# The end of a four-layer attention kernel: the last unit's exponentials, an output projection taken earlier, and unread matmuls in the last waits

## The chip, the cores and the metric

The kernel runs on one core of a Trainium2 chip. The metric is the device time of one execution in microseconds (us). The times before are three runs: 2391.03, 2398.66 and 2393.85 us, so the median is 2393.85. The profiled execution took 2389.35 us, and its span from the first to the last instruction is 2387.6 us; every time below that is a place on the profile's clock counts from the start of this span.

The engines are named as in the profile: PE is TensorE (matmuls) and PEld its weight loads, ACT is ScalarE (exponentials), DVE is VectorE (elementwise work), POOL is GpSimd and SP the engine that issues most of the transfers.

## The reference

One sequence of 2048 rows and 640 columns passes through four residual attention layers, A, B, A, B. Each has 32 heads of 20 columns. In A a query sees only the 256 keys up to itself; in B it sees all 2048.

```python
qkv = x @ wqkv                      # x normalised row by row first
scores = q @ k.T * (Dh ** -0.5)     # per head
p = softmax(scores)                 # A: only where 0 <= i - j < 256
o = p @ v
return o.reshape(B, S, D) @ wo

x = x + A(layernorm(x))
x = x + B(layernorm(x))
x = x + A(layernorm(x))
x = x + B(layernorm(x))
```

Layers are counted 0 to 3. The change touches only the end of layer 3, a full attention.

## The kernel before

**Units, banks, tiles.** The queries are cut into 4 chunks of 512 (`c`), the heads into 8 groups of 4 (`g`), the keys into 16 blocks of 128. A *unit* (l, c, g) is the attention of one chunk in one head group. The last two units are (3, 3, 6) and (3, 3, 7). A unit's scores are computed block by block: for one key block and one head of the group, one matmul (line 1186) fills one PSUM bank of 128 keys x 512 queries. Heads lie 32 rows apart, so that the matmuls of one block use different rows of TensorE. ScalarE turns three or four banks at a time into exponentials (line 1206), reading one group of banks while TensorE fills the other: banks 0 to 2 in even tiles, banks 3 to 5 or 3 to 6 in odd ones. Four-bank tiles exist only where no other work is waiting for bank 6 (`next_tile`). Their output tile is called `ka` in the profile, since it lies in an old key buffer; three-bank tiles write `pt`. A little later four matmuls (line 1238), one for each head, multiply the exponentials with the values and accumulate in bank 7 (`op`), 21 rows to a head: 20 columns of output and the sum of the exponentials.

**The side path.** In layer 3, from chunk 1 on, most units leave their last key block, number 15, to VectorE (`self.aside`). A score matmul (line 837) fills bank 6, and twelve VectorE operations (lines 843 to 881) compute the exponential of two heads from the bits of the number and a polynomial. A unit needs this twice, so 24 operations. The result is multiplied with the values by line 1247, two matmuls for each pair of heads, which end the accumulation in `op`. The planner emits these four matmuls where the unit ends, so everything behind them on TensorE waits until VectorE is done.

**The end of a unit.** `finish_unit` copies `op` to `oT` (line 805), and `t_tail` normalises it: the sums are gathered with four matmuls (line 967), their reciprocal is taken and split in two halves (lines 972 to 977), transposed (982), copied (984), spread over the heads' rows with four matmuls (991), and multiplied into `on` (995). `on` holds the normalised outputs of the 8 head groups of a chunk.

**The output projection.** `t_out` multiplies the 8 groups of `on` with `wo`, for 4 row blocks times 2 halves of the columns: 8 outputs of 8 matmuls with 320 columns (line 529), each added to x on VectorE (line 538). For the last chunk it is split: `t_before_last` takes groups 0 to 6 as soon as the tail of unit (3, 3, 6) is done (8 outputs of 7 matmuls, line 560) and adds x (line 568), into the buffer `raw_o`. `t_out` then has only group 7 left, adds `raw_o`, and stores four blocks of rows (line 544).

**What sets the order.** The order on every engine is written by a planner while the program is built: it emits one tile of scores and exponentials after another, and after each tile gives waiting tasks (`todo`, and first of all `tails`) a little work from a credit (`pump`). A task that needs a PSUM bank calls `take_m`; in this stage only bank 6 is to be had. After the last value product the planner frees banks 0 to 5 as well and emits whatever tasks are left. The planner's counts aren't times of the chip; each engine runs its instructions in the written order and waits on semaphores.

In an earlier stage, `keep_clock` (line 612) issues matmuls whose results nothing reads, so that TensorE's clock isn't lowered. It isn't used in layer 3 after chunk 0.

Of the kernel before, what the change touches and what calls it, by code (L numbers as in the profile page):

```python
# [22 lines left out]
G = 8  # L23
C = 512
NC = S // C
# [24 lines left out]
def kernel(  # L50
# [10 lines left out]
    nc = tc.nc  # L61
# [34 lines left out]
    ident = big.tile([P, P], BF16, name="ident", tag="ident")  # L96
# [3 lines left out]
    masks = big.tile([P, 3, C], BF16, name="masks", tag="masks")  # L100
# [7 lines left out]
    ps = psp.tile([P, 8, C], F32, name="ps", tag="ps")  # L108
# [20 lines left out]
    def load_wop(w):  # L129
        v = wo_in[w].rearrange("(g j e) f -> j e g f", g=G, j=4)  # L130
        for j in range(4):
            nc.sync.dma_start(out=wop[32 * j : 32 * j + DH, :, :], in_=v[j])
# [46 lines left out]
    class Task:  # L179


        count = 0

        def __init__(self, name, gen, need, left, lead):
            self.name, self.gen, self.need, self.wake = name, gen, need, 0
            self.left = left
            self.holds = False
            Task.count += 1
            self.key = (need - lead, Task.count)
# [60 lines left out]
    mfree = {5: (0, 0), 6: (0, 1)}  # L250
    mseq = [1]

    def take_m():
        while True:
            b = min(mfree, key=mfree.get)
            if mfree[b][0] <= state["tick"]:
                mfree[b] = (1 << 30, 0)
                return b
            yield ("wait", 1)

    def drop_m(b):
        mseq[0] += 1
        mfree[b] = (state["tick"] + (not state["early"]), mseq[0])
# [103 lines left out]
    def stats(l, c, i):  # L367
        if (l, c) not in mvs:
            mvs[l, c] = lnp.tile([P, 4, 2], F32, name="mv", tag="mv")
        st = lnp.tile([P, 2, 6], F32, name="stats", tag="stats")  # L370
        xv = x_sb[:, 4 * c + i, :]
        nc.vector.bn_stats(out=st[:, 0, :], in_=xv[:, 0:HD])
        nc.vector.bn_stats(out=st[:, 1, :], in_=xv[:, HD:D])
        nc.vector.bn_aggr(out=mvs[l, c][:, i, :], in_=st[:])
# [143 lines left out]
    def t_out(l, c):  # L518
        on = ons[l, c]
        last = (l, c) == (3, NC - 1)  # L520
        while last and "before_last" not in ready:
            yield ("wait", 1)
        assert out_seq[out_n[0]] == l % 2
        for qb in range(4):
            for i in range(2):
                mb = yield from take_m()
                yp = ps[:, mb, 0:HD]
                for g in range(G - 1 if last else 0, G):
                    nc.tensor.matmul(  # L529
                        yp, lhsT=on[:, g, qb * P : (qb + 1) * P],  # L530
                        rhs=wop[:, g, i * HD : (i + 1) * HD],
                        start=(last or g == 0), stop=(g == G - 1),
                    )
                    if g < G - 1:
                        yield ("hold", 0.14)
                xv = x_sb[:, 4 * c + qb, i * HD : (i + 1) * HD]
                had = part_o["t"][:, 2 * qb + i, 0:HD] if last else xv
                nc.vector.tensor_tensor(out=xv, in0=had, in1=yp, op=ALU.add)  # L538
                drop_m(mb)
                yield ("pe", 0.14)  # L540
            if l < 3:
                stats(l + 1, c, qb)
            else:
                nc.sync.dma_start(out=xout[:, 4 * c + qb, :], in_=x_sb[:, 4 * c + qb, :])
        ons.pop((l, c))
        ready.add(("out", l, c))
        ready.add(("x", l + 1, c))
        n = out_n[0] = out_n[0] + 1
        if n < len(out_seq) and out_seq[n] != out_seq[n - 1]:
            load_wop(out_seq[n])  # L550

    def t_before_last():

        on = ons[3, NC - 1]
        for qb in range(4):
            for i in range(2):
                mb = yield from take_m()
                yp = ps[:, mb, 0:HD]
                for g in range(G - 1):
                    nc.tensor.matmul(  # L560
                        yp, lhsT=on[:, g, qb * P : (qb + 1) * P],
                        rhs=wop[:, g, i * HD : (i + 1) * HD],
                        start=(g == 0), stop=(g == G - 2),
                    )
                    if g < G - 2:
                        yield ("hold", 0.14)
                xv = x_sb[:, 4 * (NC - 1) + qb, i * HD : (i + 1) * HD]
                nc.vector.tensor_tensor(
                    out=part_o["t"][:, 2 * qb + i, 0:HD], in0=xv, in1=yp, op=ALU.add
                )  # L570
                drop_m(mb)
                yield ("pe", 0.14)
        ready.add("before_last")
# [44 lines left out]
    def key_blocks(l, part):  # L618
        return part or (0, NT)

    class Unit:
        def __init__(self, l, c, g, part=None):
            self.l, self.c, self.g, self.part = l, c, g, part
            self.windowed = l % 2 == 0
            self.aside = False
            if self.windowed:
                sets = [(m, b0, subs, j) for m, b0, subs in window_banks(c) for j in range(4)]
            else:
                self.aside = l == 3 and c > 0 and (c, g) != (1, 0)
                k0, k1 = key_blocks(l, part)  # L630
                kcs = range(k0, k1 - self.aside)
                sets = [(None, 0, [(kc, 0, 4, 0)], j) for kc in kcs for j in range(4)]
            n = len(sets)
            self.banks = [
                (self, j, m, b0, subs, i < 4, i >= n - 4 and not self.aside, i == n - 1)
                for i, (m, b0, subs, j) in enumerate(sets)
            ]
# [322 lines left out]
            live["va"] -= 2 + 2 * (u.c > 0) + 2 * (u.c == NC - 1)  # L960

    def t_tail(l, c, g, on, oT):
        yield ("wait", 2)
        mb = yield from take_m()
        zp = ps[:, mb, 0:16]
        for qb in range(4):
            nc.tensor.matmul(
                zp[:, 4 * qb : 4 * qb + 4], lhsT=oT[:, qb * P : (qb + 1) * P],
                rhs=sel4[:], start=True, stop=True,
            )  # L970
        rz = rzp.tile([P, 16], F32, name="rz", tag="rz")
        nc.vector.reciprocal(out=rz[:], in_=zp)
        drop_m(mb)

        hl = rzp.tile([P, 2, 16], BF16, name="hl", tag="hl")
        nc.vector.tensor_copy(out=hl[:, 0, :], in_=rz[:])
        nc.vector.tensor_tensor(out=hl[:, 1, :], in0=rz[:], in1=hl[:, 0, :], op=ALU.subtract)
        yield ("pe", 0.25)
        yield ("wait", 2)
        mb = yield from take_m()  # L980
        rp = ps[0:32, mb, :].bitcast(BF16)[:, 0:P]
        nc.tensor.transpose(out=rp, in_=hl[:].rearrange("p n r -> p (n r)"), identity=ident[:])  # L982
        rT = rzp.tile([32, P], BF16, name="rT", tag="rT")
        nc.vector.tensor_copy(out=rT[:], in_=rp)  # L984
        drop_m(mb)
        yield ("pe", 0.1)
        yield ("wait", 2 if state["tick"] < last_tick[0] else 1)
        mb = yield from take_m()
        zb = ps[:, mb, :]
        for qb in range(4):  # L990
            nc.tensor.matmul(  # L991
                zb[:, qb * P : (qb + 1) * P], lhsT=spread4[:, qb, :], rhs=rT[:],
                start=True, stop=True,
            )
        nc.vector.tensor_tensor(out=on[:, g, :], in0=oT[:], in1=zb, op=ALU.mult)  # L995
        drop_m(mb)
        yield ("pe", 0.3)
        ready.add(("tail", l, c, g))
        if (l, c, g) == (3, NC - 1, G - 2):
            push("before_last", t_before_last(), 0, 8.0)  # L1000
        if g == G - 1:
            need = first_use(l + 1, c, 0) if l < 3 else len(units) + c
            push(("out", l, c), t_out(l, c), need, 9.0)
            if l < 3:
                push_layer(l + 1, c)
# [82 lines left out]
    with tc.manual_schedule():  # L1088
# [14 lines left out]
        n = 0  # L1103
# [48 lines left out]
        while ended is None or t < ended + 8:  # L1152
# [3 lines left out]
            if t < len(tiles) or banks:  # L1156
# [26 lines left out]
                for n in range(2):  # L1183
                    for i, (u, j, m, b0, subs, first, last, end) in enumerate(cur):
                        for kc, q0, qn, col in subs[n : n + 1]:
                            nc.tensor.matmul(  # L1186
                                sp[:, i, col * P : (col + qn) * P],
                                lhsT=u.k(kc, j), rhs=u.q(j, q0, qn), start=True, stop=True,
# [39 lines left out]
            if len(pts) >= 4 and pts[3][0] <= t - (3 if pts[0][3][0].windowed else 2):  # L1228
                group = [pts.popleft() for _ in range(4)]
                u, subs, end = group[0][3][0], group[0][3][4], group[3][3][7]  # L1230
                first, last = group[0][3][5:7]
# [3 lines left out]
                for n, (kc, q0, qn, col) in enumerate(subs):  # L1235
                    for _, pg, i, b in group:
# [3 lines left out]
                            lhsT=u.v(kc, j), rhs=pg[:, i, col * P : (col + qn) * P],  # L1240
                            start=(first and n == 0), stop=(last and n == len(subs) - 1),
                            skip_group_check=u.windowed,
                        )
                if end and u.aside:
                    pair = side_done(u)
                    for j in range(4):
                        nc.tensor.matmul(
                            op[32 * j : 32 * j + VW, :], lhsT=u.v(NT - 1, j),
                            rhs=pair[j // 2][:, j % 2, :], start=False, stop=True,
# [21 lines left out]
                        )  # L1271
                    i = k
            masked = (cur, pt) if n_b else None
        mfree.update((b, (0, 0)) for b in range(6))
        state["early"] = True
        while tails or todo:
            state["tick"] += 1
# [31 lines left out]
```

## Time and profile before

| what | value |
|---|---|
| median of three runs | 2393.85 us |
| span of the profiled execution | 2387.6 us |
| ScalarE busy | 2200.7 us, 92% |
| TensorE busy | 1994.0 us, 84% |
| VectorE busy | 1265.8 us, 53% |
| mean granted TensorE clock | 0.808 |
| last exponential ends | 2363.59 us |

A row of groups names the line, engine and operation, the tile written and the tiles read with their shapes, the number of instructions, their busy time and mean duration, and then the idle time just ahead of them with what ended it. A row of the timeline gives the start, the length, the same names, and in brackets the idle time of the engine ahead of it and who released it. In the slices each digit is a fortieth of the span, in tenths. A row of stretches gives from and to, the length, busy time (with the number of instructions) of PE, PEld, DVE, ACT and POOL, then the granted clock, the DMA share and GB/s.

### The profile page before, as it was taken

The numbers are of one execution on the slowest core, as the hardware profiler recorded it, in microseconds if no ns is written. First come the engines' busy times: TensorE is split into PE (matmuls) and PEld (weight loads), VectorE is DVE, ScalarE is ACT, GpSimd is POOL, SyncE is SP. The second block draws the span as 40 slices with busy tenths as digits, with TensorE's granted clock in tenths as the row PEclk, the third lists the DMA queues.
The fourth block names the chain that finished last, engine by engine and source line by source line (L and its number), as shares of the span: only waits on it lengthen the run. The fifth ranks groups of instructions, "written<-read, shape, count | busy, mean of one in ns | idle before, by whom it ended". The sixth has DMA issues, their size and how long they took to land. (4 is left out here: it accounts for less than half of the span.)

```text
span 2387.6 us, 39480 instructions
## 1 busy us (share of the span) xinstructions
PE 1994.0 (84%) x15394; PEld 705.2 (30%) x15539; DVE 1265.8 (53%) x2460; ACT 2200.7 (92%) x1738; POOL 141.2 (6%) x295
## 2 busy tenths in 40 slices
PE   7888988888888798888878888888888788888886
PEld 3443333323322332223322333232222121122112
DVE  6576776423323343423443434442577777777776
ACT  7777889899999999999999999999999999999995
POOL 3111110000000001000100001001000000000000
PEclk9899999978998998889997999789755575557556
DMA  6232422322200232102330124112210010011000
GB/s 182 71 94 70 112 67 59 81 61 65 82 19 26 57 80 83 34 13 57 87 94 16 20 82 109 33 31 76 63 29 26 26 37 26 27 38 37 26 13 12
DMA packets 173676, 132.51 MB, mean 55 GB/s; under 512 B 115760, under 2 KB 156080, under 8 KB 173488
## 3 DMA queue, kind: packets, MB, share of 16 engines
q1 hardware_dynamic: 163872, 101.39, 17.2%
q0 software_dynamic: 9616, 28.59, 3.5%
q8 instruction: 122, 2.00, 0.4%
q14 instruction: 66, 0.54, 0.1%
HBM read 98.70 MB, written 27.79 MB: 53 GB/s over the span
## 5 line engine op out<-in xcount | busy, mean ns | idle before, releaser
L1206 ACT ACTIVATE pt<-ps 128x1536 bf16<-128x1536 f32 (+3 forms) x1586 | 2054.9, 1452 | 127.0 <-PE ps L1186 113.1
L1186 PE MATMUL ps<-qt,kt 32*128 32x512 bf16 x4004 | 659.5, 476 | 230.3 <-ACT pt L1206 169.9
L1238 PE MATMUL ps<-pt,vt 128*21 128x512 bf16 x3744 | 479.2, 469 | 23.1 <-DVE oT L805 13.4
L1186 PEld LDWEIGHTS <-kt 32*128 32x128 bf16 x4004 | 191.3, 94 | 645.9 <-issue 623.6
L1268 DVE TENSOR_TENSOR pt<-pt,masks 128x1024 bf16<-128x1024 bf16 (+5 forms) x403 | 238.7, 626 | 101.8 <-ACT pt L1206 101.0
L353 PE MATMUL ps<-xnT,wqk 128*128 128x512 bf16 x761 | 217.6, 397 | 28.8 <-DMA wqk<-in_B_wqkv_dram 9.6
L1238 PEld LDWEIGHTS <-vt 128*21 128x21 bf16 x4004 | 104.0, 91 | 369.9 <-issue 361.4
L304 DVE CAST st<-ps 128x512 bf16<-128x512 f32 x127 | 87.8, 691 | 199.3 <-PE ps L353 192.3
L612 PE MATMUL ps<-masks,ident 128*128 128x512 bf16 x467 | 173.8, 435 | 4.7 <-issue 3.5
L529 PE MATMUL ps<-wop,on 128*128 128x320 bf16 x968 | 168.9, 318 | 5.9 <-DVE on L995 3.5
L1186 PE MATMUL ps<-qa,ka 32*128 32x384 bf16 (+2 forms) x1408 | 119.6, 282 | 42.7 <-ACT pt L1206 38.1
L995 DVE TENSOR_TENSOR on<-oT,ps 128x512 bf16<-128x512 bf16 x128 | 87.5, 684 | 115.6 <-PE ps L991 113.8
L538 DVE TENSOR_TENSOR x_sb<-x_sb,ps 128x320 bf16<-128x320 bf16 x120 | 58.1, 484 | 146.5 <-PE ps L529 146.3
L843 DVE TENSOR_SCALAR xnT<-ps 128x512 int32<-128x512 f32 x92 | 63.5, 691 | 128.5 <-PE ps L837 125.4
L805 DVE CAST oT<-ps 128x512 bf16<-128x512 f32 x112 | 76.8, 686 | 101.2 <-PE ps L1238 87.4
L1206 ACT ACTIVATE ka<-ps 128x2048 bf16<-128x2048 f32 x65 | 127.3, 1959 | 2.7 <-PE ps L1186 2.2
L444 PE MATMUL ps<-wv,xnT 128*128 128x320 bf16 x640 | 114.5, 313 | 5.3 <-DVE va L304 1.5
L529 PEld LDWEIGHTS <-on 128*128 128x128 bf16 x968 | 89.4, 102 | 72.9 <-issue 37.6
L353 PEld LDWEIGHTS <-wqk 128*128 128x128 bf16 x830 | 72.2, 99 | 123.4 <-issue 51.5
L1238 PE MATMUL ps<-pt,va 128*21 128x384 bf16 (+2 forms) x1408 | 80.2, 291 | 9.8 <-DVE oT L805 4.1
L1186 PEld LDWEIGHTS <-ka 32*128 32x128 bf16 x1408 | 44.3, 92 | 111.4 <-issue 103.4
L984 DVE COPY rT<-ps 32x128 bf16<-32x128 bf16 x128 | 26.8, 209 | 89.4 <-PE ps L982 88.8
(91 smaller groups left out, 1437.5 us busy)
## 6 DMA issues: line engine op xcount, KB each, us to landing
vt<-v_d SPq DMA_DIRECT2D x48, 336.0 KB
kt<-k_d SPq DMA_DIRECT2D x192, 80.0 KB
wqk<-in_B_wqkv_dram SPq DMA_DIRECT2D x80, 160.0 KB
wqk<-in_A_wqkv_dram SPq DMA_DIRECT2D x70, 160.0 KB
k_d<-st POOLq DMA_DIRECT2D x75, 128.0 KB, 2.2
q_d<-st POOLq DMA_DIRECT2D x75, 128.0 KB, 2.0
qt<-q_d SPq DMA_DIRECT2D x384, 20.0 KB
v_d<-vs POOLq DMA_DIRECT2D x16, 336.0 KB, 3.2
```

The lines of the kernel that those rows point to most:

```text
L304: nc.vector.tensor_copy(out=out_, in_=in_)
L353: nc.tensor.matmul(pq, lhsT=wt[:, dc, :], rhs=xt[:, dc, :], start=(dc == 0), stop=(dc == KD - 1),)
L444: nc.tensor.matmul(pv, lhsT=xt[:, dc, i * P : (i + 1) * P], rhs=wv_sb[l % 2][:, dc, h * HD : (h + 1) * HD], start=(dc == 0), stop=(dc == K ...
L529: nc.tensor.matmul(yp, lhsT=on[:, g, qb * P : (qb + 1) * P], rhs=wop[:, g, i * HD : (i + 1) * HD], start=(last or g == 0), stop=(g == G - 1),)
L612: nc.tensor.matmul(ps[:, b, :], lhsT=ident[:], rhs=masks[:, 0, :], start=True, stop=True)
L805: nc.vector.tensor_copy(out=oT[:], in_=op)
L843: V.tensor_scalar(out=xi.bitcast(I32)[:, i * C : (i + 1) * C], in0=ps[:, 6, :], scalar1=SCALE * LOG2E * E23, scalar2=127.0 * E23, op0=ALU. ...
L995: nc.vector.tensor_tensor(out=on[:, g, :], in0=oT[:], in1=zb, op=ALU.mult)
L1186: nc.tensor.matmul(sp[:, i, col * P : (col + qn) * P], lhsT=u.k(kc, j), rhs=u.q(j, q0, qn), start=True, stop=True,)
L1206: nc.scalar.activation(out=pt[:, i:k, b0 * P :], in_=sp[:, i:k, b0 * P :], func=ACT.Exp, scale=SCALE,)
L1238: nc.tensor.matmul(op[32 * j : 32 * j + VW, q0 * P : (q0 + qn) * P], lhsT=u.v(kc, j), rhs=pg[:, i, col * P : (col + qn) * P], start=(first ...
L1268: nc.vector.tensor_tensor(out=pt_[:, i:k, b0 * P :], in0=pt_[:, i:k, b0 * P :], in1=mv_, op=ALU.mult,)
```

## The change

Four edits, all at the end of layer 3.

- The last unit (3, 3, 7) no longer uses the side path: ScalarE computes the exponentials of its key block 15 like the others'. This is meant to take the wait for VectorE out of the end.
- `t_before_last` takes six groups instead of seven, and is started after the tail of unit (3, 3, 5) rather than (3, 3, 6). It then runs while the last units compute, and `t_out` at the end takes the two groups that are left, 16 matmuls instead of 8.
- In the last tail, `fill` issues 2, 3, 1 and 3 matmuls of 128x512 whose result nothing reads, into bank 0, in the places where TensorE waits for VectorE. They are meant to keep TensorE's clock up.
- Bank 0 is left out of the banks that are freed at the end, since the fills write there.

```diff
-                for g in range(G - 1 if last else 0, G):
+                g0 = G - 2 if last else 0
+                for g in range(g0, G):
...
-                        start=(last or g == 0), stop=(g == G - 1),
+                        start=(g == g0), stop=(g == G - 1),
...
-                for g in range(G - 1):
+                for g in range(G - 2):
...
-                        start=(g == 0), stop=(g == G - 2),
+                        start=(g == 0), stop=(g == G - 3),
...
-                    if g < G - 2:
+                    if g < G - 3:
...
-                self.aside = l == 3 and c > 0 and (c, g) != (1, 0)
+                self.aside = l == 3 and c > 0 and (c, g) not in ((1, 0), (NC - 1, G - 1))
...
     def t_tail(l, c, g, on, oT):
+        def fill(count):
+
+            for n in range(count * ((l, c, g) == (3, NC - 1, G - 1))):
+                nc.tensor.matmul(
+                    ps[:, 0, :], lhsT=ident[:], rhs=masks[:, 0, :], start=True, stop=True
+                )
+
         yield ("wait", 2)
+        fill(2)
...
         yield ("pe", 0.25)
+        fill(3)
...
         yield ("pe", 0.1)
+        fill(1)
...
         yield ("pe", 0.3)
+        fill(3)
         ready.add(("tail", l, c, g))
-        if (l, c, g) == (3, NC - 1, G - 2):
+        if (l, c, g) == (3, NC - 1, G - 3):
             push("before_last", t_before_last(), 0, 8.0)
...
-        mfree.update((b, (0, 0)) for b in range(6))
+        mfree.update((b, (0, 0)) for b in range(1, 6))
```

In the written order the two programs are the same on every engine up to the score tile after the tail of unit (3, 3, 5). From there, the eight groups of `t_before_last` follow one after another between the score tiles of unit (3, 3, 6) and the first ones of (3, 3, 7), two before and six after the second pair of side scores begins. Six of their eight adds stand ahead of the last side operation of unit (3, 3, 6) on VectorE. The last unit has 64 banks instead of 60. From the point where the orders part, the changed program has 21 exponentials of three banks, 6 of four and a last one of a single bank, where the program before has 24 of three and 3 of four.

## The prediction

> **What bounds the kernel now.** I read the page first: which engine is full, at which clock.
>
> ```profile
> PE 1994.0 (84%) x15394; PEld 705.2 (30%) x15539; DVE 1265.8 (53%) x2460; ACT 2200.7 (92%) x1738; POOL 141.2 (6%) x295
> ACT  7777889899999999999999999999999999999995
> PEclk9899999978998998889997999789755575557556
> L1206 ACT ACTIVATE pt<-ps 128x1536 bf16<-128x1536 f32 (+3 forms) x1586 | 2054.9, 1452 | 127.0 <-PE ps L1186 113.1
> ```
>
> ScalarE (ACT) is busy 92% of the span, nearly all of it in exponentials, until a last slice at half: the end is the one place where it isn't the bound. Late in the run TensorE mostly has half its clock. Since the two programs issue the same instructions in the same order on every engine up to about 2322 us, only the last 65 us can differ. So the timeline of the end:
>
> ```profile
> 2337.63 0.60 PE L1247 MATMUL ps<-ka,vt 128*21 128x512 bf16 x2 [1.72 <-DVE ka L881]
> 2338.87 14.94 ACT L1206 ACTIVATE pt<-ps 128x1536 bf16<-128x1536 f32 x11 [1.48 <-PE ps L1186]
> ...
> 2355.21 8.38 ACT L1206 ACTIVATE pt<-ps 128x1536 bf16<-128x1536 f32 x6 [1.40 <-PE ps L1186]
> ...
> 2370.07 0.69 DVE L881 TENSOR_TENSOR ka<-ka,xnT 128x1024 bf16<-128x1024 bf16 x1
> 2370.81 0.61 PE L1247 MATMUL ps<-ka,vt 128*21 128x512 bf16 x2 [4.50 <-DVE ka L881]
> ...
> 2371.46 0.69 DVE L805 CAST oT<-ps 128x512 bf16<-128x512 f32 x1 [0.70 <-PE ps L1247]
> ...
> 2380.00 0.69 DVE L995 TENSOR_TENSOR on<-oT,ps 128x512 bf16<-128x512 bf16 x1 [0.67 <-PE ps L991]
> ...
> 2380.75 2.31 PE L529 MATMUL ps<-wop,on 128*128 128x320 bf16 x8 [0.78 <-DVE on L995]
> 2381.23 3.27 DVE L538 TENSOR_TENSOR x_sb<-raw_o,ps 128x320 bf16<-128x320 f32 x8 [0.54 <-PE ps L529]
> 2382.14 2.72 SPq L544 DMA_DIRECT2D out_dram<-x_sb  x4
> ```
>
> The last exponential ends at 2355.21 + 8.38 = 2363.59; the span ends at 2387.6, so 24.0 us follow without ScalarE. First the side path (the exponential of key block 15 on VectorE, lines 843 to 881) holds TensorE 4.50 us at L1247. Then the last unit's normalization takes 2371.46 to 2380.7, stretched by leftover groups of `t_before_last` (L560) between its steps. Last come eight adds and the stores. The other wait matters too: at 2337.63 the same L1247 of the unit before cost ScalarE 1.48 us.
>
> The clock, and what an output projection costs between exponentials, I took from stretches:
>
> ```profile
> 2350.00:2355.00 5.00, 4.92 (x28) 1.67 (x24) 3.49 (x7) 3.81 (x3) 0.00 (x0) 0.50 0.00 0
> 2355.00:2360.00 5.00, 4.31 (x36) 1.54 (x34) 3.45 (x6) 4.69 (x4) 0.00 (x0) 0.96 0.00 0
> ```
>
> ```profile
> 2155.67 2.12 PE L529 MATMUL ps<-wop,on 128*128 128x320 bf16 x8
> ...
> 2158.37 1.26 PE L529 MATMUL ps<-wop,on 128*128 128x320 bf16 x8
> 2158.54 1.45 ACT L1206 ACTIVATE pt<-ps 128x1536 bf16<-128x1536 f32 x1 [0.78 <-PE ps L1186]
> ```
>
> The first shows clock 0.50 turning into 0.96 once L560 groups run (the clock is the column before the DMA share). The second is an earlier output projection: its groups held ScalarE up 0.78 us.
>
> **What the Trainium skill says.** "TensorE: Matmul & The Clock Gate", Part 1, says the clock doubles after a busy activity window of about 3.4 us and falls after an idle one. The trace agrees for full 128x128 matmuls (changes near 2355.2, 2369.0, 2375.8 and 2379.3, some 3.4 us or multiples apart), but "busy" isn't the record: scores and value products kept TensorE 80% busy at 0.50 for hundreds of us. The same page, Part 2, says matmuls stay in program order; the trace agrees, at L1247 ready scores stand behind a blocked product. "PSUM — Partial Sum Buffer", section Engine vs sequencer instructions, says VectorE's queue is strictly first in, first out; so an add put among the side operations delays every later one.
>
> **The change, part by part.** Times are on the profile's clock; the streams part at the exponential that starts at 2322.57.
>
> *Exponentials.* A 3-bank exponential comes every 1.35 us (14.94 less one duration of 1.47, over 10), a 4-bank one takes 1.76 until the next. From 2322.57 the kernel before has 24 and 3 of them: 24 x 1.35 + 3 x 1.76 = 37.7 of 41.0 us elapsed. After: 21 and 6 and a single bank (0.65 by the mean of that form): 28.4 + 10.6 + 0.6 = 39.6 us. That is 4 banks more, the last unit's block 15, +1.9 us on ScalarE's path.
>
> *Removed from the end.* The last unit's 24 side operations and their wait go, as do the leftover groups inside the last normalization.
>
> *Moved: `t_before_last` a unit earlier.* Its eight groups, now of six matmuls, stand from 2322 on between the exponentials of the last unit but one. In half clock a matmul of 320 columns takes 0.27 us, so a group 1.62; a score set and a product set 0.54 each; together 2.7 us in a tile against 1.35 of exponential. In full clock: 0.15 x 6 + 0.65 = 1.55 (2158.37 to 2159.56 for eight). I walked the new order with these. Group 1 starts with `on` at 2321.95, so the next scores come 0.8 late. Group 2 costs 0.3 to 1.35, by when the clock turns up; I take 0.3, as such a stretch turned it up before. Then come two side scores without groups, no loss, but about 6 us without full matmuls, so groups 3 and 4 start at half clock again. Groups 3 to 6 lose 1.1 (0 to 1.5). Ten 3-bank exponentials are then done by 2322.57 + 13.5 + 2.2 = 2338.3.
>
> *The wait this lengthens.* Of the adds of `t_before_last` (0.49 us), four now lie between the side operations of the last unit but one, and three of them first wait for their group, 0.3 to 0.5 us each. Before, the chain from its second L843 to L881 took 2328.26 to 2337.57, 9.3 us. Now: about the same start (2328.4), plus 4 x 0.53 + 1.2, ends 2341.1. L1247's second pair waits for that, and the eleventh tile's scores stand behind it: product and scores 0.4 + 0.6, so ScalarE resumes at 2342.1, after 3.8 us idle where it was 1.48. Groups 7 and 8, cold again after that idle time, lose 1.4 (0.5 to 2.3). Nothing after that is slower than ScalarE: a 4 and a 3 tile took 3.11 us in just such a stretch.
> Losses 0.8 + 0.3 + 1.1 + 3.8 + 1.4 = 7.4; last exponential ends at 2322.57 + 39.6 + 7.4 = 2369.6, 6.0 later than before.
>
> *The new end.* From the rows of before: last value product to end of the L805 copy 1.2 to 1.4; sums (L967) and three small VectorE steps 1.0; transpose and copy 0.5; spread 0.3; the multiply until the first output matmul 1.3 to 1.4: 4.1 at full clock. From L529's start to the end 6.85 was measured (2380.75 to 2387.6). Sum 11.0. The nine unread matmuls cost nothing at full clock, since 3 x 0.22 lie beside the 0.7 us of small VectorE steps or the multiply. At half clock (0.43 each) three take 1.3 and hold the transpose up 0.5 and the output 0.45; and two matmuls an output at 0.54 then outrun the adds' 0.41 spacing, +1.2. All cold: 13.2. The fills should turn the clock up partway; I take 12.0. Changing the PSUM bank list costs nothing, as the other banks are free by then.
>
> *Sum.* -24.0 + 12.0 + 6.0 = -6.0 us; 2393.85 - 6.0 = 2387.9.
>
> **The rivals.**
> *A, overlap is nearly free:* the clock is up before group 1's end and stays up. For: 2155 to 2166 stayed up through its groups. Against: 6 us of side scores without full matmuls between groups 2 and 3. ScalarE resumes at 2340.8, groups 7 and 8 lose 0.5, end 11.0: -9.2 us, 2384.7.
> *B, the overlap eats the gain:* clock down throughout groups 3 to 6 pushes the adds and so the side chain; resume at 2344, end 13.2: -2.9 us, 2391. For: every stretch without groups since 2200 ran at 0.50. Against: groups turned it up each time.
> *C, slower:* the side wait recurs for each remaining group or the cold output misses still more. It would need 6 us more loss than I found, e.g. each group waiting a side operation (8 x 1.2): about +3.6, 2397.5. Against: adds stand between side operations in groups' order, and TensorE never waited over 0.6 us for one.
>
> **How the numbers follow.** Forecast 0.52, A 0.26, B 0.17, C 0.05. The bound of 0.3% is 7.2 us; the three times before already lie 7.6 apart (2391.03 to 2398.66), so the measured median shifts by some 2 to 3 us by itself. Faster by over 0.3%: 0.85 of A, a third of the forecast, little of B: 0.40. Slower: most of C, 0.04. The rest 0.56. Range: A's end less noise to B's with it, 2382.5 to 2393.
>
> **What would show it.** Right: ScalarE resumes near 2342 behind a wait of 3 to 4.5 us for L881's counterpart, its last exponential ends at 2368 to 2371 (single bank), some 12 us from there to the end, no side operation for the last unit. Wrong: an idle under 2 us at that wait (A), an exponential ending past 2372, or an end over 14 us long.

## The result, and the profile after

Four timed runs of the changed kernel have a median of 2380.97 us (2379.77 to 2383.09), four of the kernel before 2396.26 us (2391.03 to 2401.44): ratio 0.9937, 95% interval 0.9912 to 0.9962. That is 15.3 us less where 6 were forecast, and 2380.97 lies just under the stated range. The profiles say something else. Their spans are 2387.6 and 2381.4 us, a difference of 6.2, and even that isn't the effect, since the part that both programs share took 2.7 us longer in the profile after. To leave the shared part out I count from a landmark, the last one that all kernels here have in common: the normalization output (`on`) of unit (3, 3, 4). Before, then after:

```profile
2292.42 0.68 DVE L995 TENSOR_TENSOR on<-oT,ps 128x512 bf16<-128x512 bf16 x1
```

```profile
2295.11 0.67 DVE L1006 TENSOR_TENSOR on<-oT,ps 128x512 bf16<-128x512 bf16 x1
```

From there to the end of the span are 95.2 us before and 86.3 after: **the end became 8.9 us shorter**. Below, "the end" is this stretch.

The page after, as far as it answers to the lines shown of before:

```profile
PE 1989.8 (84%) x15402; PEld 705.7 (30%) x15548; DVE 1246.9 (52%) x2436; ACT 2200.6 (92%) x1739; POOL 141.5 (6%) x295
ACT  6787889899999999999999999999999989999997
PEclk9898999988988999889988999789755565556557
L1218 ACT ACTIVATE pt<-ps 128x1536 bf16<-128x1536 f32 (+3 forms) x1584 | 2050.6, 1444 | 135.4 <-PE ps L1198 121.1
```

VectorE lost 24 operations and 19 us, and ScalarE's last slice, which covers all of the last 60 us, went from half to 7 tenths. (The 8 seven slices ahead of it lies at 1905 to 1965 us, in the shared part; the change doesn't reach there.) What the change costs ScalarE is within that last slice, and shows in the timeline of the end after:

```profile
2327.42 1.33 PE L561 MATMUL ps<-wop,on 128*128 128x320 bf16 x6
2327.59 1.45 ACT L1218 ACTIVATE pt<-ps 128x1536 bf16<-128x1536 f32 x1 [0.98 <-PE ps L1198]
...
2329.51 10.93 ACT L1218 ACTIVATE pt<-ps 128x1536 bf16<-128x1536 f32 x8 [0.46 <-PE ps L1198]
...
2334.02 0.99 PE L561 MATMUL ps<-wop,on 128*128 128x320 bf16 x6
...
2342.13 0.69 DVE L882 TENSOR_TENSOR ka<-ka,xnT 128x1024 bf16<-128x1024 bf16 x1
2342.87 0.39 PE L1259 MATMUL ps<-ka,vt 128*21 128x512 bf16 x2 [2.63 <-DVE ka L882]
...
2343.69 2.79 ACT L1218 ACTIVATE pt<-ps 128x1536 bf16<-128x1536 f32 x2 [3.25 <-PE ps L1198]
...
2345.08 0.97 PE L561 MATMUL ps<-wop,on 128*128 128x320 bf16 x6 [0.26 <-DVE raw_o L569]
...
2346.81 5.48 ACT L1218 ACTIVATE pt<-ps 128x1536 bf16<-128x1536 f32 x4 [0.33 <-PE ps L1198]
...
2369.35 0.77 ACT L1218 ACTIVATE pt<-ps 128x512 bf16<-128x512 f32 x1
...
2373.76 0.69 DVE L1006 TENSOR_TENSOR on<-oT,ps 128x512 bf16<-128x512 bf16 x1 [0.47 <-PE ps L1002]
2374.50 2.33 PE L530 MATMUL ps<-wop,on 128*128 128x320 bf16 x16
2374.97 3.27 DVE L539 TENSOR_TENSOR x_sb<-raw_o,ps 128x320 bf16<-128x320 f32 x8 [0.52 <-PE ps L530]
2375.89 2.71 SPq L545 DMA_DIRECT2D out_dram<-x_sb  x4
```

A group of `t_before_last` is one row of L561 (the second, third and last of the eight stand here). Read the brackets of ScalarE: it idles 0.98 and 0.46 us for the first two groups, then nothing for the next four, 3.25 us at the side product of unit (3, 3, 6), and 0.33 for the last two. The last exponential ends at 2370.12; 11.3 us follow where 24.0 did. The clock in three stretches of it (column before the DMA share):

```profile
2325.00:2330.00 5.00, 5.00 (x34) 1.71 (x32) 3.03 (x6) 3.56 (x4) 0.00 (x0) 0.68 0.00 0
2330.00:2335.00 5.00, 2.99 (x28) 1.32 (x25) 3.85 (x6) 5.00 (x5) 0.00 (x0) 1.00 0.00 2
...
2340.00:2345.00 5.00, 2.20 (x20) 0.88 (x14) 3.90 (x6) 1.75 (x2) 0.00 (x0) 1.00 0.01 3
```

It goes up during the second group and stays up, through 5.3 us without a group (2328.75 to 2334.02, scores and value products alone) and through the idle time at 2340 to 2343.

### The profile page after: what moved, and what is told of

It reads as the page before. It is cut to its first block, busy times and chain, and to the rows that moved or that the text cites. A ratio compares the mean times of both kernels' runs of the same rounds, so it can differ in the third digit from the quotient of the medians.

```text
span 2381.4 us, 39470 instructions
## 1 busy us (share of the span) xinstructions
PE 1989.8 (84%) x15402; PEld 705.7 (30%) x15548; DVE 1246.9 (52%) x2436; ACT 2200.6 (92%) x1739; POOL 141.5 (6%) x295
## 5 line engine op out<-in xcount | busy, mean ns | idle before, releaser
L1218 ACT ACTIVATE ka<-ps 128x2048 bf16<-128x2048 f32 x68 | 133.2, 1959 | 2.6 <-PE ps L1198 2.1
L1198 PEld LDWEIGHTS <-ka 32*128 32x128 bf16 x1408 | 44.8, 92 | 111.5 <-issue 103.5
L1250 PE MATMUL ps<-ka,vt 128*21 128x512 bf16 x272 | 69.7, 597 | 2.6 <-DVE oT L806 1.9
```

The lines of the kernel that those rows point to most:

```text
L1198: nc.tensor.matmul(sp[:, i, col * P : (col + qn) * P], lhsT=u.k(kc, j), rhs=u.q(j, q0, qn), start=True, stop=True,)
L1218: nc.scalar.activation(out=pt[:, i:k, b0 * P :], in_=sp[:, i:k, b0 * P :], func=ACT.Exp, scale=SCALE,)
L1250: nc.tensor.matmul(op[32 * j : 32 * j + VW, q0 * P : (q0 + qn) * P], lhsT=u.v(kc, j), rhs=pg[:, i, col * P : (col + qn) * P], start=(first ...
```

## The experiments

Every run has its own profile, so every end could be measured apart from its total. Line numbers of the kernels made from the changed one are the changed one's (6 higher behind the condition that grew in late_lag). Each figure is rounded by itself to 0.1.

| kernel | end, us | of it up to the last exponential | after it | ratio to before, 95% |
|---|---|---|---|---|
| before, before_copy | 95.2, 95.3 | 71.2 | 24.0 | 0.999 (0.997 to 1.001) |
| after, after_copy | 86.3, 86.3 | 75.0 | 11.3 | 0.9957 (0.9938 to 0.9975) |
| act_only | 86.4 | 75.0 | 11.4 | 0.9966 (0.9947 to 0.9986) |
| early_only | 89.7 | 73.0 | 16.7 | 0.9975 (0.9956 to 0.9994) |
| no_fill | 87.2 | 74.7 | 12.6 | 0.9960 (0.9932 to 0.9988) |
| late_six, late_six_again | 85.4, 85.4 | 73.9 | 11.5 | 0.9957 (0.9939 to 0.9975), the second |
| no_side_two | 87.1 | 74.1 | 13.0 | 0.9953 (0.9934 to 0.9972) |
| late_no_side | 86.1 | 74.1 | 11.9 | 0.9958 (0.9941 to 0.9976) |
| late_lag | 83.9 | 72.0 | 11.9 | 0.9926 (0.9898 to 0.9954) |

The texts on record count, mostly, from unit (3, 3, 5)'s output, which lies 28.8 us after the landmark above where both orders still agree (66.4 and 57.5 us for 95.2 and 86.3).

**Both kernels once more, unchanged.**

> The kernel before, unchanged, once more with its own profile. From the output of the normalization of unit (3, 3, 5) to the end of the span its first profile has 66.4 us, the changed kernel's 57.5, a gain of 8.9, while the medians differ by 15. Theory 1 (the end alone, and spread): the time up to that point differs from run to run by several us in both kernels, so this copy has 65 to 68 us in its end, and whatever its total differs by lies ahead. Theory 2 (an unlucky clock at the end): the first profile was a lucky one, and the end of the kernel before mostly takes 70 us or more, since its leftover projection groups run at half clock.

> The changed kernel, unchanged, on the same chip as the kernel before. Theory 1: 7 to 11 us faster than the kernel before when the rounds are interleaved; end of 56 to 59 us. Theory 2: 13 us or more faster, end of 56 to 59 us against 70 or more. Recorded forecast of 6 us: the end would have to be near 60 us.

Before: end 95.3 us, in a span of 2383.6. After: end 86.3 again, in a span of 2397.0. The ends repeat to 0.1 us while the totals wander by over 10: theory 1. Timed on one chip, 22 runs of the changed kernel have a median of 2382.23 and 63 of the one before 2392.21, 10.0 us apart. The interval of the ratio reaches from 6.0 to 14.8 us: it holds the 8.9 of the ends, and not the 15.3 of the first medians. Theory 2 falls, since the copy takes 66.5 us from unit (3, 3, 5)'s output and not 70 or more.

Where the rest comes from: up to the landmark the programs issue the same instructions, yet of the twelve profiles the one of early_only gets there in 2285.99 us and the one of no_side_two in 2311.06. The stretch from the start to the landmark in these two (weight loads 15122 in both, ScalarE within 6 us):

```profile
0.00:2285.99 2285.99, 1940.16 (x15122) 684.35 (x15122) 1201.73 (x2363) 2129.78 (x1691) 141.66 (x295) 0.82 0.22 58
```

```profile
0.00:2311.06 2311.06, 1982.19 (x15122) 685.25 (x15122) 1202.21 (x2363) 2135.20 (x1691) 141.21 (x295) 0.80 0.21 57
```

TensorE's busy time is 42 us longer in the slow one and its granted clock lower. Over the twelve profiles the time to the landmark goes with the time at half clock (807 to 930 us of it; correlation 0.92, about 0.22 us for each us), and over the 63 timed runs of the kernel before the time goes with the mean granted clock (correlation -0.83). That the clock causes it is likely, but only these correlations stand behind it.

**The first edit alone.**

```diff
-                self.aside = l == 3 and c > 0 and (c, g) != (1, 0)
+                self.aside = l == 3 and c > 0 and (c, g) not in ((1, 0), (NC - 1, G - 1))
```

> The first edit alone: the last unit wholly on ScalarE, seven groups taken after unit (3, 3, 6), no unread matmuls. Theory 1: the wait of 4.5 us for VectorE and the leftover groups leave the end, four more banks cost 1.9 us, and the projection groups cost some 3 us between exponentials: 7 to 9 us faster than before, so nearly all of the change. Rival: the early start is what brings the gain, and this edit alone gives 4 us or less.

End 86.4: 8.8 of the 8.9 us. The other three edits together bring 0.2 on top of it. This one line does two things at once: the wait for VectorE goes, and all eight groups now lie ahead of the last exponential (2358.39 to 2372.71), where before three of the eight lay behind it. The runs don't say how much of the 8.8 us is due to each. Its groups of seven, in the last unit, cost ScalarE 1.22, 0.56, 0.26, 0.26, 0.56 and 0.26 us, with 1.48 at the side product:

```profile
2350.79 9.56 ACT L1206 ACTIVATE pt<-ps 128x1536 bf16<-128x1536 f32 x7 [1.48 <-PE ps L1186]
2361.56 2.83 ACT L1206 ACTIVATE pt<-ps 128x1536 bf16<-128x1536 f32 x2 [1.22 <-PE ps L1186]
2364.95 1.45 ACT L1206 ACTIVATE pt<-ps 128x1536 bf16<-128x1536 f32 x1 [0.56 <-PE ps L1186]
```

**The early groups alone**, by an edit to the changed kernel.

```diff
-                self.aside = l == 3 and c > 0 and (c, g) not in ((1, 0), (NC - 1, G - 1))
+                self.aside = l == 3 and c > 0 and (c, g) != (1, 0)
...
-            for n in range(count * ((l, c, g) == (3, NC - 1, G - 1))):
+            for n in range(0):
```

> The early groups alone: six groups after unit (3, 3, 5), two at the end, the last unit keeps its side path, no unread matmuls. If the wait for VectorE at the end is what the change removes, it stays here with some 4 us after the last exponential, and the stall of unit (3, 3, 6) comes on top: an end of 60 to 62 us against 66.4 before and 57.5 changed. Rival, taking the groups out of the end is what gains: 58 us or less.

End 89.7, which counted from (3, 3, 5) is 60.9: as expected. So taking the groups out of the last normalization is worth 5.5 us by itself: 7.3 us less behind the last exponential, 1.8 more ahead of it. It overlaps with what the first edit alone brings, and the wait for VectorE stays. That wait is the first row here; the other two are the last outputs:

```profile
2363.19 0.60 PE L1259 MATMUL ps<-ka,vt 128*21 128x512 bf16 x2 [3.55 <-DVE ka L882]
...
2367.63 4.42 PE L530 MATMUL ps<-wop,on 128*128 128x320 bf16 x16 [0.78 <-DVE on L1006]
2368.36 4.22 DVE L539 TENSOR_TENSOR x_sb<-raw_o,ps 128x320 bf16<-128x320 f32 x8 [0.78 <-PE ps L530]
```

This kernel has no unread matmuls, and TensorE is at half clock: its 16 output matmuls take 4.42 us against 2.33 in the changed kernel, and the adds behind them 4.22 against 3.27.

**The change without its unread matmuls.**

```diff
-            for n in range(count * ((l, c, g) == (3, NC - 1, G - 1))):
+            for n in range(0):
```

> The change without its nine unread matmuls. Read from the output of the normalization of unit (3, 3, 5) to the end of the span, 57.4 to 57.5 us with them. If they raise the clock for the last outputs: TensorE stays at half clock, 16 output matmuls at 0.27 us outrun the adds, and the end is 1 to 2 us longer (58.5 to 59.5). Rival, they do nothing that shows: 57 to 58, or a little shorter than with them.

End 87.2, 0.9 longer (58.4 from (3, 3, 5), just under what was expected), all of it after the last exponential: 12.6 against 11.3, less 0.3 gained ahead of it. The unread matmuls do raise the clock: without them the 16 output matmuls take nearly twice the 2.33 us that they take in the changed kernel.

```profile
2366.80 4.43 PE L530 MATMUL ps<-wop,on 128*128 128x320 bf16 x16 [0.78 <-DVE on L1006]
```

They just about pay for the eight more output matmuls that the change puts at the end; act_only, with eight fewer there and none unread, needs 11.4.

**The groups late again.**

```diff
-        if (l, c, g) == (3, NC - 1, G - 3):
+        if (l, c, g) == (3, NC - 1, G - 2):
             push("before_last", t_before_last(), 0, 8.0)
```

> The change with t_before_last pushed after unit (3, 3, 6) again, still six groups and still with the unread matmuls. The adds then no longer stand between side operations. Theory 1: the idle time of 3.25 us at the side product of unit (3, 3, 6) is back at about 1.5, ScalarE loses 1 to 3 us less ahead of it, and the groups lose about the same in the last unit: equal to the change or up to 2 us faster. Rival (the early start pays): 2 to 4 us slower than the change, since the groups crowd the last unit.

> The late six groups once more, beside it on the same chip, since the earlier run had few timed executions. Its end takes 85.4 us again, to 0.1 us, and whatever its total differs by lies ahead of the end. Timed, 9 to 10 us faster than the kernel before; the rival is that the 13 us of its earlier ratio were real, which an end of under 83 us would have to show.

End 85.4 both times, 0.9 shorter than the change. The idle time at the side product is back at 1.48:

```profile
2341.95 9.56 ACT L1218 ACTIVATE pt<-ps 128x1536 bf16<-128x1536 f32 x7 [1.48 <-PE ps L1198]
```

and the groups cost 0.79, 0.33, 0.12, 0.12, 0.33 and 0.35, together 2.0. In the change the groups cost nearly as much, 1.8 (0.98, 0.46 and 0.33), and their adds on VectorE lengthen the wait at the side product by 1.8 besides. So starting `t_before_last` early doesn't pay. The first run's ratio (10 runs) was 0.9946 and the second's (22) 0.9957, with the same end.

**The side path taken from two units.**

```diff
-                self.aside = l == 3 and c > 0 and (c, g) not in ((1, 0), (NC - 1, G - 1))
+                self.aside = l == 3 and c > 0 and (c, g) not in ((1, 0), (NC - 1, G - 2), (NC - 1, G - 1))
```

> The change, and unit (3, 3, 6) wholly on ScalarE as well: 4 more banks, 1.8 us more of exponentials, no VectorE chain for the early adds to delay. If the idle time of 3.25 us at the side product is the early start's price, it goes away: end of 55 to 56.5 us against 57.5. Rival, the idle time only moves (the groups then hold ScalarE up instead): 57.5 or more.

> As the run before, with the groups pushed after unit (3, 3, 6): none of the two last units uses the side path and the groups lie in the last unit. Late groups with the side path had 56.6 us, of which 1.5 were the stall of unit (3, 3, 6), at 1.8 us less of exponentials: so 56.5 to 57.2 expected. Rival (a unit freed of the side path runs better than its exponentials say): 55 us or less.

The orders part before unit (3, 3, 5)'s output here, so only the end from (3, 3, 4) compares. With early groups it is 87.1, 0.8 longer than the change where at least 1 less was expected; with late groups 86.1, 0.7 longer than late_six, at the upper edge. The first expectation failed. The stall did go (last exponential 0.9 earlier), but 13.0 us follow the last exponential. The last tile now has three banks instead of one, and the clock turns up 6.0 us after the last exponential, where in the change it turns up after 2.4. late_no_side, with three banks and the clock up after 3.3 us, needs 11.9; so the late rise is the likely cause, but no run changes it alone. With late groups the four banks of exponentials cost a little more than the wait they remove: the last exponential ends 0.2 later than in late_six.

**The side product one tile later**, on top of the late groups.

```diff
-            if len(pts) >= 4 and pts[3][0] <= t - (3 if pts[0][3][0].windowed else 2):
+            if len(pts) >= 4 and pts[3][0] <= t - (
+                3
+                if pts[0][3][0].windowed or (
+                    pts[3][3][7] and pts[3][3][0] is units[index[3, NC - 1, G - 2, None]]
+                )
+                else 2
+            ):
```

> The late six groups, and the side product of unit (3, 3, 6) emitted one tile later, so that one more set of scores stands ahead of it on TensorE. From the output of the normalization of unit (3, 3, 4) to the end: 95.2 us before, 86.3 changed, 85.4 with the late groups. If the 1.48 us idle time at that product is only its place in the order, it is gone and the end takes 83.9 to 84.5 us. Rival, VectorE is still too late a tile later, or the values product behind it holds the next scores up: 85 us or more.

End 83.9, as expected. One more set of scores stands ahead of the product, and the row below, the counterpart of the one with 1.48 above, carries no idle time:

```profile
2344.36 1.98 ACT L1218 ACTIVATE ka<-ps 128x2048 bf16<-128x2048 f32 x1
2346.11 9.63 ACT L1218 ACTIVATE pt<-ps 128x1536 bf16<-128x1536 f32 x7
```

This version beats both kernels, by 11.4 us of the end against before and 2.4 against the change. Timed, its seven runs have a ratio of 0.9926, 17.7 us, with an interval of 11 to 24; the end explains 11.4.

## Why the prediction was wrong

*Exponentials, 39.6 us:* right. From the first that differs (about 2325.3) to 2370.12 are 44.8 us, of which 5.0 idle, so 39.8.

*Groups 1 and 2, 0.8 + 0.3:* right in kind; 0.98 + 0.46. The clock turned up within the second.

*"groups 3 and 4 start at half clock again", and "groups 7 and 8, cold again after that idle time":* this step failed. The clock stayed up from 2328.2 to 2352.1. Groups 3 to 6 cost nothing instead of 1.1, groups 7 and 8 together 0.33 instead of 1.4. The prediction put the gap without groups at about 6 us and let the clock fall in it without a measured case; the gap was 5.3, and the clock held in all four profiles with this order (after, after_copy, no_fill, early_only). The profile of before had shown such a case. These are two groups of its last unit, with side scores and no group between them:

```profile
2355.03 1.30 PE L560 MATMUL ps<-wop,on 128*128 128x320 bf16 x7
...
2361.28 1.12 PE L560 MATMUL ps<-wop,on 128*128 128x320 bf16 x7
```

That is a gap of 4.9 us (2356.33 to 2361.28) with the clock up throughout; the prediction's own row from 2355 to 2360, with 0.96, lies across most of it. On the clock rival A was right, and it came nearest as a whole: counted on the profile of before (2.7 us less), ScalarE resumed at 2341.0 where A had 2340.8 and the forecast 2342.1. But A's sign, an idle time under 2 us, didn't come, and the clock turned up in the second group and not in the first.

*The lengthened wait, 3.8:* right in kind, 3.25, and shown by late_six, where it is 1.48. VectorE's chain took 11.3 us (2331.48 to 2342.82) and not 12.7: its adds waited 0.48 us for their groups, where 1.2 was assumed at half clock.

*The new end, 12.0:* 11.3, within the 11.0 to 13.2 given, as are the 12.6 without the unread matmuls. These turned the clock up at 2372.5, 2.0 us ahead of the first output matmul. One sum of this part was off: the steps listed ahead of the first output matmul add up to 4.3 to 4.6 us and not to 4.1; 4.4 were measured (2370.12 to 2374.50).

*Sum:* the losses were mis-sized by 2.4 us (7.4 forecast, 5.0 measured), mostly by the failed step, and the end by 0.7; the exponentials took 0.2 more. So the profiles give -8.9 and not -6.0.

*"the measured median shifts by some 2 to 3 us by itself":* too small, and this put the first measurement outside the range: 8.9 us off the median of before, 2393.85 or 2396.26, would have been 2385.0 or 2387.4, well inside. The 63 runs of the kernel before have a standard deviation of 6.9 us. A median of four drawn from them scatters by 3.8, a difference of two such medians by 5.3. The 6.4 us by which 15.3 exceeds 8.9 is 1.2 of these. That it is such chance is supported by the repeats (10.0 us on 22 and 63 runs), but not shown run by run, as only one run of each kernel was profiled then.

Rival B had the clock down throughout groups 3 to 6, and it was up; of C nothing showed.

## What to carry to other kernels

Where the shared part of a program wanders by more than the effect, measure the changed stretch from a landmark that both programs have: here it repeated to 0.1 us, while totals of the same kernel differed by over 15. Ask what each edit gives alone: one line gave 8.8 of 8.9 us, while starting the projection early cost 0.9 against starting it late, because its short adds were put into a chain on VectorE that TensorE waits for in order. Such a wait can be cheaper to hide, by one more tile of ready work ahead of it (1.5 us), than to remove.

## What the runs showed of the hardware

The clock changes of the end lie at multiples of 3.41 us from each other: after, at 2328.15, 2352.05, 2372.53 and 2379.35, which are 7, 6 and 2 times 3.41 apart. So the end can be cut into windows of this length, and the time that the groups' matmuls (128x128 weights, 320 columns) take in each window can be read off. Up to the last exponential this sorts every window of the twelve profiles in which the clock was up: it stayed up after each with 0.59 us or more of them, and fell after each with 0.43 us or less. The gap of 5.3 us lies across two windows, 2328.15 to 2331.56 and 2331.56 to 2334.98, with 0.60 and 0.96 us; the next window without any is 2348.63 to 2352.05, and at its end the clock fell, although TensorE was busy for 1.69 us of it with other matmuls. In late_six the last group leaves 0.43 us in its last window, so the fall came 3.0 us after it, and in the change 6.0. How long a gap may be thus depends on where it lies.

Scores and value products alone didn't raise the clock: in the profile after it stayed at half from 2184.79 to 2328.15 with TensorE busy 81% of the time. The first groups raised it 2.0 to 3.6 us after their start, after windows with 1.77 us or more of them; 1.1 and 1.2 us weren't enough (in the two profiles of before, behind the last exponential). As matmuls take nearly twice as long at half clock (4.43 against 2.33 us for the sixteen above), this doesn't show that fewer of them hold the clock than raise it. Nor is the time in a window all that counts: before, from 2375.91 to 2379.32, behind the last exponential, a window with 1.45 us of full matmuls and hardly anything else ended in a fall.
